# Attention over pooled keys and values, then four weighted experts: turning the probabilities on VectorE in 32x32 blocks, two heads as one element

## The chip, the cores and the metric

One core of a Trainium2 chip runs the whole program. The metric is device time in microseconds (us) from launch to end. The core has five engines that each work through a list of their own in order and wait for one another by semaphores: TensorE (PE; its weight loads are shown as PEld), VectorE (DVE), ScalarE (ACT), GpSimd (POOL) and SyncE (SP). POOL and SP issue the transfers between the memory of the chip (HBM) and the core. Matrix products are made in PSUM, all else lies in SBUF, which has 128 partitions.

## What is computed

```python
B, H, S, D = 8, 8, 576, 64                 # q, k, v; float32
k_p = k.reshape(B, H, 72, 8, D).mean(axis=3)
v_p = v.reshape(B, H, 72, 8, D).mean(axis=3)
scores = D ** -0.5 * (q @ k_p.transpose(0, 1, 3, 2))
attn = exp(scores - max(scores)); attn /= attn.sum() + 1e-9      # over the last axis
x = (attn @ v_p).transpose(0, 2, 1, 3).reshape(4608, 512)
p = domain_probs / (domain_probs.sum(-1) + 1e-9)                 # 4608 x 4
out = sum(p[:, e] * (relu(x @ w1[e]) @ w2[e]) for e in range(4)) # w1: 512 x 1024, w2: 1024 x 512
```

## The kernel before

The 4608 tokens are 36 tiles of 128; four tiles are a group of 512. An expert of a group is a *step*: 9 groups x 4 experts = 36 steps. A step has 12 *slots*, in threes: two slots with an `up` (L545, 4 products of 512 columns into `h_ps`, then a Relu on ScalarE, L549), always for the next step, and one slot with a `down` (L577, 8 products of 512 columns into `o_ps`) for one tile of this step, and its `collect` on VectorE (L592, or L588 for the first expert), which weighs `o_ps` and adds it to `acc`. `h_ps` and `o_ps` have two PSUM buffers each. The tiles of attention are done between these products: `plan` holds for each slot the functions to call after the slot's product, and `plan_tile` and `plan_batch` fill it. The order on every engine is the order in which the program calls things; no scheduler changes it.

For tile t, `due` is the first slot of its group and `base = due - 14` from tile 8 on. The functions and their slots after base are:

- `turn_q` (0): brings the queries to head dimension by token. From tile DT = 9 on this is VectorE's 32x32 transpose (L385) of `qblk`, which the load has already cut into blocks; earlier tiles do it on TensorE.
- `scores` (2): 4 products, one for each pair of heads, against `kT`, the turned sums of keys; head c and head c + 4 are a pair, on 64 partitions each. `less_max` (2) on VectorE: row maxima (L421) and their subtraction (L428).
- `expo` (4) on ScalarE (L446); it puts the heads back into order while it writes.
- `normalise` (5) on VectorE: row sums (L465), two short instructions (L454, L459), the product with the reciprocals into `ebuf` (L467), as bf16, 8 heads x 72 = 576 values a token.
- `turn_e` (8): TensorE turns `ebuf` in 5 blocks of 128 columns (the last one half empty) into `eT_ps` (L363), ScalarE copies them to `eT` (L364).
- `context_turned` (10): 8 products (L528) of `eT` with `vblk`, the sums of values spread with a mask so that each product gives the outputs of two neighbouring heads; then ScalarE's copy to `xT` (L533).

Tile 4 (`TPG`) to tile 7 are planned with other slots in steps 1 and 2, tiles 0 to 3 are written out by hand ahead of the steps. `gather_q` copies the queries of tiles 5 to 8 out of one wide load, in the slot ahead of their `turn_q`.

A batch has 576 tokens, 4.5 tiles. `plan_batch` spreads over slots, relative to the base of the first tile that needs the batch: `fold_k` twice and `end_k` (base - 6, - 5, - 4; sums of eight key rows on VectorE, L275 and L285, into `kpad`), `turn_k` (base - 2; TensorE, L304, then two copies, L312), `fold_v` twice, `end_v`, `spread_v` (base + 2 to + 5; L275, L325, L331). A load of the batch after next follows as soon as the buffer is free (`load_k`, `load_v`, L98; `load_qblk`, L149), all through POOL's queue. A tile that lies in two batches does its products in two segments.

Of the kernel before, what the change touches and what calls it, by code (L numbers as in the profile page):

```python
# [9 lines left out]
ACT = mybir.ActivationFunctionType  # L10
# [7 lines left out]
def kernel(  # L18
# [31 lines left out]
    NZ = 4  # L50
    BLK = 32
    PW = 2 * SP
    assert H * D == DM and D == 64 and SP == 72 and P == 128 and TAIL == 64

    const = ctx.enter_context(tc.tile_pool(name="const", bufs=1))
    wpool = ctx.enter_context(tc.tile_pool(name="wpool", bufs=1))
    raw = ctx.enter_context(tc.tile_pool(name="raw", bufs=1))
    prep = ctx.enter_context(tc.tile_pool(name="prep", bufs=2))
    qpool = ctx.enter_context(tc.tile_pool(name="qpool", bufs=8))
    qtpool = ctx.enter_context(tc.tile_pool(name="qtpool", bufs=TPG))  # L60
    qbpool = ctx.enter_context(tc.tile_pool(name="qbpool", bufs=2))
    soft = ctx.enter_context(tc.tile_pool(name="soft", bufs=2))
# [9 lines left out]
    ctx.enter_context(tc.manual_schedule())  # L72

    kraw = [raw.tile([P, NB, POOL * D], BF16, name=f"kraw{i}") for i in range(2)]
    vraw = [raw.tile([P, NB, POOL * D], BF16, name=f"vraw{i}") for i in range(2)]
    ebuf = [raw.tile([P, NB * P], BF16, name=f"ebuf{i}") for i in range(2)]
    w1_sb = [wpool.tile([P, KC, F], BF16, name=f"w1_{e}") for e in range(E)]
    w2_sb = [wpool.tile([P, FB, DM], BF16, name=f"w2_{e}") for e in range(E)]
# [22 lines left out]
        load_rows(nc.gpsimd, kraw[b % 2], rows_of(k[b]))  # L101

    def load_v(b):
        load_rows(nc.gpsimd, vraw[b % 2], rows_of(v[b]))

    def segments(t0, n):
        segs = []
        t = t0
        while t < t0 + n:
            b = t // S  # L110
            end = min(t0 + n, (b + 1) * S)
            segs.append((b, t - b * S, end - t, t - t0))
            t = end
        return segs


    qrow, qblk = {}, {}
# [26 lines left out]
    def load_qblk(b):  # L144

        qblk[b] = qbpool.tile([P, NPAIR * (S // BLK), BLK], BF16, name="qblk")
        for n32 in range(P // BLK):
            z, half = divmod(n32, 2)
            nc.gpsimd.dma_start(  # L149
                out=qblk[b][n32 * BLK:(n32 + 1) * BLK],  # L150
                in_=q[b][z * NPAIR:(z + 1) * NPAIR, :, half * BLK:(half + 1) * BLK]
                .rearrange("c (a i) j -> i (c a) j", i=BLK),
            )

    def load_w1(e, halves=(0, 1)):
        for half in halves:
# [11 lines left out]
            )  # L168

    qrun = raw.tile([P, 2, NPAIR, TPG, D], BF16, name="qrun")  # L170
    k0 = raw.tile([P, NB, POOL * D], F32, name="k0")
    load_rows(nc.sync, k0, rows_of(k[0]), ((NB - 1, NB), (0, 2), (2, NB - 1)))

    qg = raw.tile([P, H, TPG, D], F32, name="qg")
# [22 lines left out]
    for sign, base in ((1, PW), (-1, -SP - 1)):  # L197
        nc.gpsimd.affine_select(
            out=own[:], in_=own[:], compare_op=ALU.is_ge, fill=0.0,
            base=base, channel_multiplier=sign,  # L200
            pattern=[[sign * (P - PW), NB], [-sign * SP, NZ]],
        )
    gate = const.tile([1, 1], F32, name="gate")

# [36 lines left out]

    MZ = NZ - 1
    mask_v = const.tile([P, NB, MZ, D], BF16, name="mask_v")

    def spread_mask():
        nc.scalar.copy(
            out=mask_v[:], in_=own[:, :, 1:NZ].unsqueeze(3).to_broadcast([P, NB, MZ, D])
        )

    def domain_probs(probs, t0, t1):  # L250
        dsum = const.tile([P, t1 - t0], F32, name=f"dsum{t0}")
# [45 lines left out]
    def turn_k(b, odd=None, order=range(NB), between={}):  # L297

        flat = pads[b][:].rearrange("p i z d -> p (i z d)")
        ps = ps_t.tile([P, NB * P], BF16, tag="t", name="kT_ps")  # L300
        for i in order:

            n = P if i < NB - 1 or b > 0 else TAIL
            nc.tensor.transpose(  # L304
                ps[:, i * P:i * P + n], flat[0:n, i * P:(i + 1) * P], ident[0:n, 0:n]
            )
            if i in between:
                warm(between[i])
        kT[b] = kTs[b % 2]
        for z, copy in ((0, nc.scalar.copy), (1, odd or nc.scalar.copy)):  # L310
            half = slice(z * D, (z + 1) * D)
            copy(  # L312
                out=kT[b][half].rearrange("x (c z j) -> x z c j", z=2, j=SP)[:, z],
                in_=ps[half, 0:ROWS].rearrange("x (z c j) -> x z c j", z=2, j=SP)[:, z],
            )

    vsum = {}

    def fold_v(b, n):
        fold(vraw[b % 2], 0, NB, n)  # L320

    def end_v(b):
        rows = vraw[b % 2]
        vsum[b] = prep.tile([P, NB, D], BF16, name="v_sum")
        nc.vector.tensor_add(  # L325
            out=vsum[b][:], in0=rows[:, :, 0:D], in1=rows[:, :, D:2 * D]
        )

    def spread_v(b):
        vblk[b] = vblks[b % 2]  # L330
        nc.vector.tensor_tensor(  # L331
            out=vblk[b][:, :, 1:NZ],
            in0=vsum[b][:].unsqueeze(2).to_broadcast([P, NB, MZ, D]),
            in1=mask_v[:], op=ALU.mult,
        )
# [60 lines left out]
    def scores(t, halves=False):  # L396
        if halves:
            banks = [ps_h.tile([P, 512], F32, tag="h", name="sch")[:] for _ in range(2)]
            scs[t] = [(bank, slice(i, i + 1)) for i, bank in enumerate(banks)]
        else:  # L400
            sc = ps_s.tile([P, 2, 512], F32, name="sc")
            banks = [sc[:, 0, :], sc[:, 1, :]]
            scs[t] = [(sc[:].rearrange("p g x -> p (g x)"), slice(0, 2))]
        for b, _, n, at in segments(t * P, P):
            for pair in range(NPAIR):
                nc.tensor.matmul(  # L406
                    banks[pair // 2][at:at + n, (pair % 2) * PW:(pair % 2 + 1) * PW],
                    lhsT=qT[t][:, pair, at:at + n],
                    rhs=kT[b][:, pair * PW:(pair + 1) * PW],
                )  # L410

    maxima = {}
# [26 lines left out]
    def expo(t):  # L439

        if t < TPG:
            e = ebuf[t % 2][:, 0:ROWS]
        else:
            ef[t] = soft.tile([P, ROWS], F32, name="e_sb")
            e = ef[t][:]
        nc.scalar.activation(  # L446
            out=e.rearrange("p (z c j) -> p c z j", z=2, j=SP),
            in_=ds.pop(t)[:].rearrange("p g (c z) j -> p (g c) z j", z=2),
            func=ACT.Exp, scale=EXP_SCALE,
        )  # L450
# [11 lines left out]
    def normalise(t):  # L462
        e = ef.pop(t)[:].rearrange("p (h j) -> p h j", j=SP)
        total = soft.tile([P, H], F32, name="total")
        nc.vector.reduce_sum(out=total[:], in_=e, axis=AX.X)  # L465
        inverse(t, total[:])
        nc.vector.tensor_tensor(  # L467
            out=ebuf[t % 2][:, 0:ROWS].rearrange("p (h j) -> p h j", j=SP), in0=e,
            in1=es.pop(t)[:].unsqueeze(2).to_broadcast([P, H, SP]), op=ALU.mult,
        )  # L470

    def turn_e(t, copy=None):
        eT[t] = soft.tile([P, NB, P], BF16, name="eT")
        e = ebuf[t % 2]
        turned(eT[t][:], [e[:, i * P:(i + 1) * P] for i in range(NB)], "eT", copy)

# [44 lines left out]
    def context_turned(t):  # L523
        ps = ps_t.tile([P, KC, P], F32, tag="t", name="xT_ps")
        for b, _, n, at in segments(t * P, P):
            for pair in range(NPAIR):
                for i, z0 in ((pair, 2), (pair + 1, 0)):
                    nc.tensor.matmul(  # L528
                        ps[:, pair, at:at + n],
                        lhsT=vblk[b][:, i, z0:z0 + 2].rearrange("p z d -> p (z d)"),  # L530
                        rhs=eT[t][:, i, at:at + n], start=(z0 == 2), stop=(z0 == 0),
                    )
        nc.scalar.copy(out=x_columns(t), in_=ps[:])  # L533
# [95 lines left out]
    def plan_batch(b, slot, turn_slot, v_slot):  # L629
        at(slot, fold_k, b, 4)  # L630
        at(slot + 1, fold_k, b, 2)
        at(slot + 2, end_k, b)
        at(turn_slot, turn_k, b)
        at(v_slot, fold_v, b, 4)
        at(v_slot + 1, fold_v, b, 2)
        at(v_slot + 2, end_v, b)
        at(v_slot + 3, spread_v, b)
        if b + 2 < B:
            at(slot + 3, load_k, b + 2)
            at(v_slot + 3, load_v, b + 2)  # L640

    def plan_tile(t, base, steps):
        if TPG < t < DT:
            at(base - 1, gather_q, t)
        at(base, turn_q, t)
        at(base + steps[0], scores, t)
        at(base + steps[0], less_max, t)
        at(base + steps[1], expo, t)
        at(base + steps[2], normalise, t)
        at(base + steps[3], turn_e, t)  # L650
        at(base + steps[4], context_turned, t)
        return base + steps[4] + 1

# [3 lines left out]
    plan_batch(1, 3, 7, 18)  # L657
    for t in range(TPG, 2 * TPG):
        assert plan_tile(t, 12 + 3 * (t - TPG), (3, 5, 6, 9, 11)) <= 3 * SLOTS - 2
    last_b = 1  # L660
    for t in range(2 * TPG, NT):
        due = (t - TPG) * SLOTS
        base = due - 14
        b = ((t + 1) * P - 1) // S
        if b > last_b:
            plan_batch(b, base - 6, base - 2, base + 2)
            if 2 < b < B - 1:
                at(base + 1, load_qblk, b + 1)
            last_b = b
        assert plan_tile(t, base, (2, 4, 5, 8, 10)) <= due - 3  # L670

# [85 lines left out]
    down(0, 1)  # L759
    collect(0, 1)  # L760
    up_tile(0, 3, (0,))
    load_k(2)
    load_qblk(2)
    load_v(2)
# [46 lines left out]
```

## Time and profile before

| what | value |
|---|---|
| median of 3 runs | 560.41 us (560.26 to 561.49) |
| the profiled execution | 560.3 us |
| its span, first to last instruction | 558.6 us |
| mean granted TensorE clock | 0.999 |
| L545 `up` products | 270.4 us busy, 1084 recorded |
| L577 `down` products | 268.1 us busy, 1122 recorded |
| L363 transposes of probabilities, TensorE | 15.9 us busy, 180 |
| L528 products of the context | 19.6 us busy, 288 |
| L364 copy of turned probabilities, ScalarE | 24.1 us busy, 35 |
| period of an ordinary tile, collect to collect | 14.79 us (300.18 to 314.97) |

The span is what the profile sees; the time of a run has about 1.7 us around it. A matmul's recorded duration includes the way through the array and overlaps the next one, so counts times durations is more than the span; what a product costs TensorE is seen from the start of one to the start of the next. In a timeline each line has the start, the duration, the engine, the line of the program and, in square brackets, how long the engine sat idle before it and who released it.

### The profile page before, as it was taken

How to read it: one execution, taken by the hardware profiler on the slowest of the kernel's cores; microseconds unless marked ns; L12 is line 12 of the kernel's file. 1: busy time of each engine (PE TensorE's matmuls, PEld its weight loads, DVE VectorE, ACT ScalarE, POOL GpSimd, SP SyncE). 2: the span in 40 equal slices, each digit the busy share in tenths (PEclk: the TensorE clock that was granted, in tenths of full speed). 3: DMA queues.
4: the chain of work that ended last, by engine and by line, in shares of the span. 5: the costliest groups of instructions: out<-in, count | busy, mean ns of one | idle time of the engine just before them, and what ended most of it. 6: DMA issues, size and time to landing. Idle time of an engine off the chain costs nothing.

```text
span 558.6 us, 7696 instructions
## 1 busy us (share of the span) xinstructions
PE 547.1 (98%) x3187; PEld 277.6 (50%) x3245; DVE 275.7 (49%) x475; ACT 251.8 (45%) x435; POOL 62.5 (11%) x83
## 2 busy tenths in 40 slices
PE   7999999999999999999999999999999999999997
PEld 5854545444444445444444444544444444444444
DVE  5636846444654446544664444654456444422223
ACT  6744645444444444444444444544454444433330
POOL 6254331000400002200050003000000000000000
PEclk9999999999999999999999999999999999999999
DMA  9999996210690011901092019101000100001002
GB/s 221 207 200 206 182 158 138 43 5 0 105 100 0 2 56 40 108 0 39 38 97 33 19 58 38 6 1 62 14 2 0 47 31 0 1 38 39 0 1 76
DMA packets 87459, 33.67 MB, mean 60 GB/s; under 512 B 62080, under 2 KB 82368, under 8 KB 87424
## 3 DMA queue, kind: packets, MB, share of 16 engines
q0 software_dynamic: 75344, 21.43, 37.5%
q1 hardware_dynamic: 12080, 11.74, 6.2%
q8 instruction: 25, 0.41, 0.3%
q14 instruction: 10, 0.08, 0.1%
HBM read 45.16 MB, written 9.44 MB: 98 GB/s over the span
## 4 chain that ended last, share of the span: by engine, by line
PE 95%; DVE 3%; issue 1%; DMA 1%; SPq 0%; ACT 0%; ACTq 0%
PE o_ps L577 44%; PE h_ps L545 42%; PE xT_ps L528 3%; PE eT_ps L363 2%; PE sc L406 2%; PE h_ps L560 1%; DMA k<-in_k_dram 1%; DVE d_sb L428 1%; DVE mx L421 0%; PE kT_ps L304 0%; DVE k L275 0%; PE last_ps L610 0%; PE x_ps L497 0%; PE qT_ps L363 0%; DVE vraw L275 0%
## 5 line engine op out<-in xcount | busy, mean ns | idle before, releaser
L545 PE MATMUL h_ps<-xT,w 128*128 128x512 bf16 x1084 | 270.4, 379 | 1.6
L577 PE MATMUL o_ps<-w,h_sb 128*128 128x512 bf16 x1122 | 268.1, 379 | 1.2
L549 ACT ACTIVATE h_sb<-h_ps 128x512 bf16<-128x512 f32 x280 | 167.2, 597 | 224.0 <-PE h_ps L545 208.5
L577 PEld LDWEIGHTS <-h_sb 128*128 128x128 bf16 x1144 | 111.8, 98 | 134.2
L592 DVE SCALAR_TENSOR_TENSOR acc<-o_ps,p_sb,acc 128x512 f32<-128x512 f32 x107 | 80.3, 751 | 189.7 <-PE o_ps L577 186.7
L545 PEld LDWEIGHTS <-w 128*128 128x128 bf16 x1120 | 105.5, 98 | 109.5
L588 DVE TENSOR_SCALAR acc<-o_ps,p_sb 128x512 f32<-128x512 f32 x36 | 27.0, 750 | 68.9 <-PE o_ps L577 68.8
L533 ACT CAST xT<-xT_ps 128x512 bf16<-128x512 f32 x32 | 18.7, 585 | 50.3 <-PE xT_ps L528 50.3
L149 POOL DMA_DIRECT2D qblk<-in_q_dram x24 | 26.8, 1126 | 59.4 <-DVE qT L385 53.3
L421 DVE TENSOR_REDUCE mx<-sc 128x8 f32<-128x576 f32 x34 | 25.7, 756 | 8.3 <-PE sc L406 8.3
L98 POOL DMA_DIRECT2D kraw<-in_k_dram x14 | 9.2, 659 | 171.3 <-DVE kpad L285 165.4
L428 DVE TENSOR_TENSOR d_sb<-sc,mx 128x576 f32<-128x576 f32 x34 | 25.8, 757 | 1.2
L446 ACT ACTIVATE e_sb<-d_sb 128x576 f32<-128x576 f32 x32 | 21.8, 683 | 6.6 <-DVE d_sb L428 3.9
L467 DVE TENSOR_TENSOR ebuf<-e_sb,rs 128x576 bf16<-128x576 f32 x32 | 24.2, 758 | 1.1
L364 ACT COPY eT<-eT_ps 128x640 bf16<-128x640 bf16 x35 | 24.1, 687 | 1.2 <-PE eT_ps L363 1.2
L465 DVE TENSOR_REDUCE total<-e_sb 128x8 f32<-128x576 f32 x32 | 23.8, 744 | 0.4 <-ACT e_sb L446 0.4
L528 PEld LDWEIGHTS <-vblk 128*128 128x128 bf16 x288 | 17.3, 98 | 7.5
L528 PE MATMUL xT_ps<-eT,vblk 128*128 128x128 bf16 (+1 forms) x288 | 19.6, 213 | 0.0
L385 DVE STREAM_TRANSPOSE qT<-qblk 128x512 bf16<-128x512 bf16 (+1 forms) x30 | 19.1, 645 | 0.0
L363 PEld LDWEIGHTS <-ebuf 128*128 128x128 bf16 x180 | 12.9, 98 | 8.2 <-ACT ebuf L446 0.7
L363 PE MATMUL eT_ps<-ident,ebuf 128*128 128x128 bf16 x180 | 15.9, 219 | 0.2 <-ACT ebuf L446 0.2
L406 PEld LDWEIGHTS <-qT 128*128 128x128 bf16 (+1 forms) x160 | 11.1, 100 | 8.8 <-DVE acc L592 0.8
(77 smaller groups left out, 187.2 us busy)
## 6 DMA issues: line engine op xcount, KB each, us to landing
out_dram<-acc SPq DMA_DIRECT2D x35, 256.0 KB, 2.0
w<-in_moe_w_dram POOLq DMA_DIRECT2D x12, 512.0 KB, 14.0
vraw<-in_v_dram POOLq DMA_DIRECT2D x8, 512.0 KB, 6.6
kraw<-in_k_dram POOLq DMA_DIRECT2D x7, 512.0 KB, 6.8
qblk<-in_q_dram POOLq DMA_DIRECT2D x24, 144.0 KB, 7.1
w<-in_moe_w_dram POOLq DMA_DIRECT2D x2, 1024.0 KB, 17.7
k<-in_k_dram SPq DMA_DIRECT2D x2, 512.0 KB, 4.6
qg<-in_q_dram SPq DMA_DIRECT2D x2, 512.0 KB, 7.0
```

The source lines that it names most:

```text
L149: nc.gpsimd.dma_start(out=qblk[b][n32 * BLK:(n32 + 1) * BLK], in_=q[b][z * NPAIR:(z + 1) * NPAIR, :, half * BLK:(half + 1) * BLK] .rearran ...
L363: nc.tensor.transpose(ps[:, i, :], block, ident[:])
L364: (copy or nc.scalar.copy)(out=dst, in_=ps[:])
L421: nc.vector.reduce_max(out=mx[:], in_=view, axis=AX.X)
L428: nc.vector.tensor_tensor(out=ds[t][:, g], in0=view, in1=mx[:].unsqueeze(3).to_broadcast([P, n, 4, SP]), op=ALU.subtract,)
L467: nc.vector.tensor_tensor(out=ebuf[t % 2][:, 0:ROWS].rearrange("p (h j) -> p h j", j=SP), in0=e, in1=es.pop(t)[:].unsqueeze(2).to_broadcas ...
L528: nc.tensor.matmul(ps[:, pair, at:at + n], lhsT=vblk[b][:, i, z0:z0 + 2].rearrange("p z d -> p (z d)"), rhs=eT[t][:, i, at:at + n], start= ...
L545: nc.tensor.matmul(ps[:], lhsT=w1_sb[e][:, kc, fb * P:(fb + 1) * P], rhs=xT[g][:, kc, :], start=(kc == 0), stop=(kc == KC - 1),)
L549: nc.scalar.activation(out=hs[s][:, fb, :], in_=ps[:], func=ACT.Relu)
L577: nc.tensor.matmul(ps[:], lhsT=hs[s][:, fb, i * P:(i + 1) * P], rhs=w2_sb[e][:, fb, :], start=(fb == 0), stop=(fb == FB - 1),)
L588: nc.vector.tensor_scalar_mul(out=accs[t][:], in0=ps[:], scalar1=p_sb[:, e, t:t + 1])
L592: nc.vector.scalar_tensor_tensor(out=accs[t][:], in0=ps[:], scalar=p_sb[:, e, t:t + 1], in1=accs[t][:], op0=ALU.mult, op1=ALU.add,)
```

## The change

From tile 9 on, VectorE turns the probabilities, and TensorE and ScalarE no longer do.

- `normalise` writes `ehalf`: 288 rows of two values, the two being neighbouring heads (2s, 2s+1) at the same pooled key. Two bf16 values side by side are read as one 4-byte element. The row of 288 is made of 9 blocks of 32.
- `turn_e_part(t, a)` takes the 32 tokens 32a to 32a+31 and turns these blocks with four instructions. Instruction r takes the blocks r, r + 4, r + 8 and writes them to partitions 32r to 32r + 31: 3 blocks for r = 0, 2 for the others, 96 or 64 elements a partition. Four parts, 16 instructions a tile, in slots base + 6 to base + 9. `eT` is then 128 partitions x 3 chunks x 128 tokens x 2 heads.
- The order of the rows of values becomes that of the 288: `load_v` from batch 2 on brings them in four transfers (not two), two heads beside each other in the 6 (not 5) places of a partition; `fold_v` runs over 6 places, `end_v` sums to `v_half`, `spread_v` makes `vh` in four instructions (not one) with a new mask. The last place of a partition is cleared once by `clear_v`.
- `context_turned` still does 8 products for a segment: two for each pair of heads, with every second element of `eT` as the streamed operand.
- The pairs of heads change: in batches from 2 on, heads 4g + 2y and 4g + 2y + 1 share partitions of queries and keys. `load_qblk` takes 8 transfers (not 4), the copies in `turn_k` and the slices in `scores` follow, and `expo` writes its input in its order.
- From tile 9 on `base` is `due - 15` (before: 14), with steps (2, 4, 5, 6, 11), so that the context is at the same slot as before, and the batches' slots move with it. The gathers of tiles 5 to 8 move to slots 13 to 16 (before 14, 17, 20 and 33).
- Room: the buffer of the first keys, `k0`, is used again as `late`, which holds `ehalf`, `eTh` and `kTh`, two of each; six instructions of ScalarE clear parts of them and of `vh` in slots 2 to 7, four more spread the mask in slot 1, two clear the sixth place of `vraw`. `qpool` has 5 buffers, not 8.

```diff
@@ load_v @@
+        if b < WB:
+            load_rows(nc.gpsimd, vraw[b % 2], rows_of(v[b]))
+            return
+        rows = rows_of(v[b]).rearrange("(g y r) x -> r g y x", g=2, y=2)
+        to = vraw[b % 2][:].rearrange("p (c y) x -> p c y x", y=2)
+        n = HR // 2
+        for c, p0, g, r0, r1 in (
+            (0, 0, 0, 0, P), (1, 0, 0, P, n), (1, n - P, 1, 0, 2 * P - n),
+            (2, 0, 1, 2 * P - n, n),
+        ):
+            nc.gpsimd.dma_start(out=to[p0:p0 + r1 - r0, c], in_=rows[r0:r1, g])
@@ spread_v @@
+        if b >= WB:
+            vblk[b] = vh[b % 2]
+            for n, (c, g) in enumerate(SPAN):
+                z = n % 2
+                nc.vector.tensor_tensor(
+                    out=vblk[b][:, n, :, z:],
+                    in0=vsum[b][:, c].unsqueeze(2).to_broadcast([P, 2, 2 - z, D]),
+                    in1=mask_h[:, n, z:].unsqueeze(1).to_broadcast([P, 2, 2 - z, D]),
+                    op=ALU.mult,
+                )
+            return
@@ normalise @@
+        if t >= DT:
+            nc.vector.tensor_tensor(
+                out=ehalf[t % 2][:, 0:HR].rearrange("p (s j) y -> p s y j", j=SP),
+                in0=e.rearrange("p (s y) j -> p s y j", y=2),
+                in1=es.pop(t)[:].rearrange("p (s y) -> p s y", y=2).unsqueeze(3)
+                .to_broadcast([P, NPAIR, 2, SP]), op=ALU.mult,
+            )
+            return
@@ new @@
+    def turn_e_part(t, a):
+        eT[t] = eTh[t % 2]
+        toks = slice(a * BLK, (a + 1) * BLK)
+        src = ehalf[t % 2][toks].rearrange("p r y -> p (r y)").bitcast(F32)
+        for r in range(P // BLK):
+            rows = slice(r * BLK, (r + 1) * BLK)
+            dst = eT[t][rows].rearrange("p c k y -> p (c k y)").bitcast(F32)
+            n = -(-(NW - r) // 4)
+            nc.vector.transpose(
+                out=dst.rearrange("p (c k) -> p c k", k=P)[:, 0:n, toks],
+                in_=src.rearrange("p (c k) -> p c k", k=P)[:, 0:n, rows],
+            )
@@ context_turned @@
+            if t >= DT:
+                for pair in range(NPAIR):
+                    g, y = divmod(pair, 2)
+                    for m in (2 * g, 2 * g + 1):
+                        nc.tensor.matmul(
+                            ps[:, pair, at:at + n],
+                            lhsT=vblk[b][:, m, y].rearrange("p z d -> p (z d)"),
+                            rhs=eT[t][:, SPAN[m][0], at:at + n, y],
+                            start=(m == 2 * g), stop=(m == 2 * g + 1),
+                        )
+                continue
@@ plan_tile @@
-        if TPG < t < DT:
-            at(base - 1, gather_q, t)
...
-        at(base + steps[3], turn_e, t)
+        if t < DT:
+            at(base + steps[3], turn_e, t)
+        else:
+            for a in range(P // BLK):
+                at(base + steps[3] + a, turn_e_part, t, a)
@@ the plan @@
+    for t in range(TPG + 1, DT):
+        at(t + 8, gather_q, t)
...
-        base = due - 14
+        base = due - (15 if t >= DT else 14)
...
-        assert plan_tile(t, base, (2, 4, 5, 8, 10)) <= due - 3
+        steps = (2, 4, 5, 6, 11) if t >= DT else (2, 4, 5, 8, 10)
+        assert plan_tile(t, base, steps) <= due - 3
@@ ahead of the steps @@
+    late = early.tile([P, NB, POOL * D], F32, tag="k0", name="late")
...
+    zeros = [x for i in range(2) for x in (
+        kTh[i][:], eTh[i][:, 2], vh[i][:, 1::2, :, 0]
+    )]
+    for t in vraw:
+        nc.scalar.memzero(t[:, NB, :])
+    at(1, spread_mask_h)
+    for i, x in enumerate(zeros):
+        at(2 + i, nc.scalar.memzero, x)
```

More of the change, by code (lines that the diff above doesn't have):

```diff
@@ L52 @@
     PW = 2 * SP
+    WB = 2
+    HR = ROWS // 2
+    NW = HR // BLK
+    SPAN = ((0, 0), (1, 0), (1, 1), (2, 1))
     assert H * D == DM and D == 64 and SP == 72 and P == 128 and TAIL == 64
@@ L57 @@
     raw = ctx.enter_context(tc.tile_pool(name="raw", bufs=1))
+    early = ctx.enter_context(tc.tile_pool(name="early", bufs=1))
     prep = ctx.enter_context(tc.tile_pool(name="prep", bufs=2))
-    qpool = ctx.enter_context(tc.tile_pool(name="qpool", bufs=8))
+    qpool = ctx.enter_context(tc.tile_pool(name="qpool", bufs=5))
     qtpool = ctx.enter_context(tc.tile_pool(name="qtpool", bufs=TPG))
@@ L74 @@
     kraw = [raw.tile([P, NB, POOL * D], BF16, name=f"kraw{i}") for i in range(2)]
-    vraw = [raw.tile([P, NB, POOL * D], BF16, name=f"vraw{i}") for i in range(2)]
+    vraw = [raw.tile([P, NB + 1, POOL * D], BF16, name=f"vraw{i}") for i in range(2)]
+    ehalf, eTh, kTh = [], [], []
+    vh = [raw.tile([P, len(SPAN), 2, 2, D], BF16, name=f"vh{i}") for i in range(2)]
     ebuf = [raw.tile([P, NB * P], BF16, name=f"ebuf{i}") for i in range(2)]
@@ L103, in load_v @@
     def load_v(b):
-        load_rows(nc.gpsimd, vraw[b % 2], rows_of(v[b]))
+        if b < WB:
[9 more added lines that the diff above has]
+            nc.gpsimd.dma_start(out=to[p0:p0 + r1 - r0, c], in_=rows[r0:r1, g])
     def segments(t0, n):
@@ L147, in load_qblk @@
         for n32 in range(P // BLK):
[L148 to L153, printed above, removed]
+            y, half = divmod(n32, 2)
+            to = qblk[b][n32 * BLK:(n32 + 1) * BLK].rearrange("i (g c) d -> i g c d", g=2)
+            for g in range(2):
+                head = 4 * g + 2 * y
+                nc.gpsimd.dma_start(
+                    out=to[:, g],
+                    in_=q[b][head:head + 2, :, half * BLK:(half + 1) * BLK]
+                    .rearrange("z (a i) d -> i (z a) d", i=BLK),
+                )
     def load_w1(e, halves=(0, 1)):
@@ L170 @@
     qrun = raw.tile([P, 2, NPAIR, TPG, D], BF16, name="qrun")
-    k0 = raw.tile([P, NB, POOL * D], F32, name="k0")
+    k0 = early.tile([P, NB, POOL * D], F32, tag="k0", name="k0")
     load_rows(nc.sync, k0, rows_of(k[0]), ((NB - 1, NB), (0, 2), (2, NB - 1)))
@@ L201 @@
             pattern=[[sign * (P - PW), NB], [-sign * SP, NZ]],
+        )
+    ownh = const.tile([P, 3, 2, 2], BF16, name="ownh")
+    nc.gpsimd.memset(ownh[:], 1.0)
+    for sign, base in ((1, 0), (-1, SP - 1)):
+        nc.gpsimd.affine_select(
+            out=ownh[:], in_=ownh[:], compare_op=ALU.is_ge, fill=0.0,
+            base=base, channel_multiplier=sign,
+            pattern=[[sign * P, 3], [-sign * PW, 2], [-sign * SP, 2]],
         )
@@ L243 @@
     mask_v = const.tile([P, NB, MZ, D], BF16, name="mask_v")
+    mask_h = const.tile([P, len(SPAN), 2, D], BF16, name="mask_h")
     def spread_mask():
@@ L248, in spread_mask, with spread_mask_h @@
         )
+    def spread_mask_h():
+        for n, (c, g) in enumerate(SPAN):
+            nc.scalar.copy(
+                out=mask_h[:, n], in_=ownh[:, c, g].unsqueeze(2).to_broadcast([P, 2, D])
+            )
     def domain_probs(probs, t0, t1):
@@ L308, in turn_k @@
                 warm(between[i])
-        kT[b] = kTs[b % 2]
+        kT[b] = kTs[b % 2] if b < WB else kTh[b % 2]
         for z, copy in ((0, nc.scalar.copy), (1, odd or nc.scalar.copy)):
             half = slice(z * D, (z + 1) * D)
+            if b >= WB:
+                copy(
+                    out=kT[b][half, z].rearrange("x (g r) -> x g r", g=2),
+                    in_=ps[half, 0:ROWS].rearrange("x (g y r) -> x y g r", g=2, y=2)[:, z],
+                )
+                continue
             copy(
@@ L317, with clear_v @@
     vsum = {}
+    def clear_v(b):
+        nc.scalar.memzero(vraw[b % 2][BLK:TAIL, NB - 1, :])
     def fold_v(b, n):
-        fold(vraw[b % 2], 0, NB, n)
+        fold(vraw[b % 2], 0, NB if b < WB else NB + 1, n)
     def end_v(b):
         rows = vraw[b % 2]
+        if b >= WB:
+            vsum[b] = prep.tile([P, 3, 2, D], BF16, name="v_half")
+            nc.vector.tensor_add(
+                out=vsum[b][:].rearrange("p c y d -> p (c y) d"),
+                in0=rows[:, :, 0:D], in1=rows[:, :, D:2 * D],
+            )
+            return
         vsum[b] = prep.tile([P, NB, D], BF16, name="v_sum")
         nc.vector.tensor_add(
-            out=vsum[b][:], in0=rows[:, :, 0:D], in1=rows[:, :, D:2 * D]
+            out=vsum[b][:], in0=rows[:, 0:NB, 0:D], in1=rows[:, 0:NB, D:2 * D]
         )
     def spread_v(b):
+        if b >= WB:
+            vblk[b] = vh[b % 2]
+            for n, (c, g) in enumerate(SPAN):
+                z = n % 2
[4 more added lines that the diff above has]
+                    op=ALU.mult,
+                )
+            return
         vblk[b] = vblks[b % 2]
@@ L408, in scores @@
                     lhsT=qT[t][:, pair, at:at + n],
-                    rhs=kT[b][:, pair * PW:(pair + 1) * PW],
+                    rhs=kT[b][:, pair * PW:(pair + 1) * PW] if b < WB
+                    else kT[b][:, :, pair * SP:(pair + 1) * SP],
                 )
@@ L445, in expo @@
             e = ef[t][:]
+        if t >= DT:
+            nc.scalar.activation(
+                out=e, in_=ds.pop(t)[:].rearrange("p g h j -> p (g h j)"),
+                func=ACT.Exp, scale=EXP_SCALE,
+            )
+            return
         nc.scalar.activation(
@@ L466, in normalise @@
         inverse(t, total[:])
+        if t >= DT:
[4 more added lines that the diff above has]
+                .to_broadcast([P, NPAIR, 2, SP]), op=ALU.mult,
+            )
+            return
         nc.vector.tensor_tensor(
@@ L475, in turn_e @@
         turned(eT[t][:], [e[:, i * P:(i + 1) * P] for i in range(NB)], "eT", copy)
+    def turn_e_part(t, a):
[9 more added lines that the diff above has]
+                in_=src.rearrange("p (c k) -> p c k", k=P)[:, 0:n, rows],
+            )
     CHUNKS = ((0, 2, 4), (2, 0, 4), (4, 0, 2), (1, 1, 4), (3, 1, 4))
@@ L525, in context_turned @@
         for b, _, n, at in segments(t * P, P):
+            if t >= DT:
+                for pair in range(NPAIR):
[6 more added lines that the diff above has]
+                            start=(m == 2 * g), stop=(m == 2 * g + 1),
+                        )
+                continue
             for pair in range(NPAIR):
@@ L633, in plan_batch @@
         at(turn_slot, turn_k, b)
+        if WB <= b < WB + 2:
+            at(v_slot - 8, clear_v, b)
         at(v_slot, fold_v, b, 4)
@@ L761 @@
     up_tile(0, 3, (0,))
+    late = early.tile([P, NB, POOL * D], F32, tag="k0", name="late")
+    room = late[:].rearrange("p i x -> p (i x)").bitcast(BF16)
+    at0 = 0
+    for i in range(2):
+        for to, n, form in (
+            (ehalf, 6 * P, dict(pattern="p (r y) -> p r y", y=2)),
+            (kTh, 2 * HR, dict(pattern="p (y r) -> p y r", y=2)),
+            (eTh, 6 * P, dict(pattern="p (c k y) -> p c k y", c=3, y=2)),
+        ):
+            part = room[:, at0:at0 + n]
+            to.append(part.rearrange(form.pop("pattern"), **form))
+            at0 += n
+    zeros = [x for i in range(2) for x in (
[6 more added lines that the diff above has]
+        at(2 + i, nc.scalar.memzero, x)
     load_k(2)
```

## The prediction

> **What bounds the kernel now.** The first view is the page's table of engines, the second the busy time in a stretch in the middle of the run:
>
> ```profile
> span 558.6 us, 7696 instructions
> PE 547.1 (98%) x3187; PEld 277.6 (50%) x3245; DVE 275.7 (49%) x475; ACT 251.8 (45%) x435; POOL 62.5 (11%) x83
> 276.00:338.00 62.00, 61.63 (x350) 30.41 (x356) 32.45 (x54) 27.35 (x48) 7.10 (x8) 1.00 0.43 46
> ```
>
> TensorE is busy all the time at a granted clock of 1.00; VectorE and ScalarE work about half of it. So TensorE's list sets the end: work taken out of it counts fully, and so does any wait put into it. The third view is the timeline of one tile (start, duration, engine, line):
>
> ```profile
> 303.88 0.75 DVE L592 SCALAR_TENSOR_TENSOR acc<-o_ps,p_sb,acc 128x512 f32<-128x512 f32 x1 [1.04 <-PE o_ps L577]
> 304.55 0.74 DVE L465 TENSOR_REDUCE total<-e_sb 128x8 f32<-128x576 f32 x1
> 305.33 0.17 DVE L454 TENSOR_SCALAR s<-total 128x8 f32<-128x8 f32 x1
> 305.41 1.89 PE L577 MATMUL o_ps<-w,h_sb 128*128 128x512 bf16 x8
> 305.53 0.20 DVE L459 RECIPROCAL rs<-s 128x8 f32<-128x8 f32 x1
> 305.77 0.76 DVE L467 TENSOR_TENSOR ebuf<-e_sb,rs 128x576 bf16<-128x576 f32 x1
> 307.34 0.75 DVE L592 SCALAR_TENSOR_TENSOR acc<-o_ps,p_sb,acc 128x512 f32<-128x512 f32 x1 [0.81 <-PE o_ps L577]
> 308.00 0.44 PE L363 MATMUL eT_ps<-ident,ebuf 128*128 128x128 bf16 x5
> 308.28 1.03 PE L545 MATMUL h_ps<-xT,w 128*128 128x512 bf16 x4
> 308.69 0.69 ACT L364 COPY eT<-eT_ps 128x640 bf16<-128x640 bf16 x1
> ```
>
> Five transposes of probabilities hold TensorE from 308.00 to 308.28, where the next products start: 0.28 us. (A product of 512 columns takes 0.216 us from start to start: a `down` of 8 has 1.73, an `up` of 4 has 0.86.) A `collect` (L592) starts 0.20 after its `down` has issued its last product, 305.41 + 1.73 = 307.14.
>
> The fourth view is how close two VectorE instructions follow each other. First the rows by shape (count, busy us, mean ns), then lines of the timeline:
>
> ```profile
> L385 DVE STREAM_TRANSPOSE qT<-qblk 128x512 bf16<-128x512 bf16 x24 | 16.8, 701 | 0.0
> L385 DVE STREAM_TRANSPOSE qT<-qblk 128x256 bf16<-128x256 bf16 x6 | 2.3, 419 | 0.0
> 147.70 0.76 DVE L385 STREAM_TRANSPOSE qT<-qblk 128x256 bf16<-128x256 bf16 x2
> 9.57 0.71 ACT L376 CAST qrow<-qg 128x256 bf16<-128x256 f32 x2
> 9.70 0.31 DVE L312 COPY kT<-kT_ps 64x288 bf16<-64x288 bf16 x1 [0.86 <-ACT kT L312]
> 10.04 0.51 DVE L376 CAST qrow<-qg 128x256 bf16<-128x256 f32 x2
> ```
>
> Two transposes that need nothing of each other, 0.42 each, take 0.76 together: the second starts 0.08 before the first ends. The collect above (303.88 + 0.75) also overlaps `total` by 0.08. One that needs the other's result starts 0.03 after its end (304.55 + 0.74 to 305.33, roughly). The copy at 9.70 writes partitions 64 to 127, the cast behind it starts at partition 0 and needs nothing of it; its load had landed by 9.57, when ScalarE's cast of the same load began. Yet it starts 0.03 after the copy's end. It is the one pair here whose outputs start at different partitions, and it does not overlap.
>
> **The change, part by part.** All sums are made against the profiled execution, 560.3 us (span 558.6), which stands 0.1 below the median of 560.41.
>
> Removed: in tiles 9 to 35, 27 tiles, 5 transposes on TensorE, 27 x 0.28 = 7.5 us on the path, and ScalarE's copy of 0.69, which hid beside it and counts nothing. The products of the context stay 8 a tile.
>
> Added on VectorE: 16 transposes a tile, in four parts, one of 96 and three of 64 elements a partition in each. The two rows above give 137 ns + 1.10 ns an element: 243 and 207 ns. The price that matters is from start to start. Overlapped by 0.08 it is 163 and 127, a part of 0.54, a tile of 2.18. One after the other, with 0.03 between, it is 273 and 237, a part of 0.98, a tile of 3.94. Consecutive ones write partitions from 0, 32, 64 and 96 in turn, so the nearest row is the pair at 9.70, and I take 3.94. The ends for the range: with no operation under the 0.16 that those of 8 elements take, a serial one costs 0.19 (3.1 a tile); with a line through 0.163 at 8 elements and the slope of 1.10, 0.29 and 0.26 (4.3).
>
> The Trainium skill, "VectorE: DVE Perf Modes", section "Two Vector instructions with no wait between them", gives a model that says the same against this change: an instruction whose output starts in another group of 32 partitions than the last output is held until all earlier ones have finished. The pair at 9.70 agrees (+0.03 where others show -0.08); by that rule the sum is the serial one, without it the overlapped one of the rival below.
>
> An ordinary tile. In the new order TensorE has, from the end of the `down` at base+5 to the context at base+11, up, up, down twice: 2 x 3.45 = 6.90 us. In that time VectorE must start the collect (0.20 late), do it (0.67 to the next start), normalise (304.55 to 306.53, and 0.03: 2.01), do two parts, a collect (0.78), two parts, and hand over (0.04): 3.70 without the parts. Room for the 16: 3.20. Serial 3.94 misses it by 0.74; that is a wait of TensorE in each tile, larger than the 0.28 saved. Behind the context in TensorE's list stands everything, so nothing hides it.
>
> A tile in which the next batch's keys are folded (5 of them: batches 3 to 7; batch 2's fall into tile 8, which keeps the old way). The order of instructions is: part, fold of 1280 elements, part, fold of 640, collect, part, last sum, part; and `turn_k` stands in TensorE's list behind the second `up` after the second `down`, 5.18 us after the first one, so that 4.94 remain. The list up to the last sum (durations 0.82, 0.48, 0.49 from the rows of L275 and L285, 0.03 each): 0.67 + 2.01 + 3 x 0.98 + 0.85 + 0.51 + 0.78 + 0.52 = 8.28. TensorE waits 3.34 at the transposes of k. The fourth part then hides under the `down` that follows.
>
> A tile in which the values are folded (6). From 1280, 640 and 320 elements in 817, 483 and 315 ns I get 0.95, 0.55 and 0.35 for the 1536, 768 and 384 of the new layout. The first lies ahead of the row maxima and puts the second collect about 0.1 off; the four products with the mask (256, 128, 256, 128 elements; 0.28 and 0.21 by the rows of L331 and L325, overlapped) put 0.7 between collect and `total`: 0.8 more wait.
>
> Sum: -7.5 + 22 x 0.74 + 6 x 0.8 + 5 x 3.34 = -7.5 + 16.3 + 4.8 + 16.7 = +30.3: 590.6.
>
> Taken as nothing, with their bounds:
> - The early part. TensorE waited once for a gathered row, and the gathers move ahead of that: a gain of at most the 1.00 that this line shows. Against it stand ten more ScalarE instructions in slots 1 to 7 (zeros, the spread mask), where its Relus follow each other every 0.86 with 0.27 of rest: about 2.1 us in all by the rows of memzero and copy (0.29 to 0.43, overlapped by 0.1), if none of it hid.
>
> ```profile
> 56.75 0.40 PE L363 MATMUL qT_ps<-ident,qrow 128*128 128x128 bf16 x4 [1.00 <-DVE qrow L139]
> ```
>
> - The context's products read every second 2-byte element. No row shows it. Reads in runs of 64 (L342) take 219 ns at 128 columns as unbroken ones do (L528): nothing. The other end is half rate, 8 x 0.056 x 27 = 12. I see no way to a gain.
> - The exponentials and the product of `normalise` keep their 576 elements a partition; the latter writes every second 2-byte element, from float inputs that already come one at a time (758 ns).
> - POOL's queue: 8 transfers instead of 4 for a batch of queries, 4 instead of 2 for values, the same bytes. The waits of that queue are for buffers (165 us for `kpad`, 53 for `qT`), so loads start early. ScalarE's clearing of value rows ahead of a load moves it a slot at most.
>
> **The rivals.**
> - *The transposes overlap.* For it: every other independent pair; against it: the pair at 9.70. Then 2.18 fits into 3.20, the value tiles' 0.8 too, and only the k tiles wait: 0.67 + 2.01 + 3 x 0.54 + 0.74 + 0.40 + 0.67 + 0.49 = 6.60 against 4.94, 1.66 x 5 = 8.3. 560.3 - 7.5 + 8.3 = 561, from 558 to 563 with the early part.
> - *Faster.* The same, with shorter transposes: a quarter of the partitions and a stream of 64 to 96 elements could take less than the fixed 0.137. The k tiles decide: their wait is 5 x (1.66 - 12 x what a step is below 0.136), so under a mean step of 0.12 us the saving wins. At 0.09 it is 5 x 1.1 = 5.5, with most of the early gain: 557.5. Against it: no VectorE instruction here takes under 0.16.
> - *The stepped read costs half rate*: 12 more, 573 if the transposes overlap, 602 if not.
>
> **How the numbers follow.** Serial 0.58, overlapped 0.20, faster 0.15, stepped read 0.05, others (all slower) 0.02. Forecast: 590; the serial case alone runs from 570 (0.19 a step: no wait in ordinary tiles, 2.7 in the k tiles, 4 for values) to 601 (4.3 a tile). The range reaches down over the overlapped case: 557 to 600. Within 0.2% (1.1 us) is about what a measurement of this kernel can't tell from no change; the overlapped case is split 0.07 faster, 0.06 same, 0.07 slower. So faster 0.15 + 0.07 = 0.22, same 0.06, slower 0.58 + 0.07 + 0.05 + 0.02 = 0.72.
>
> **What would show it.** Right: starts of the transposes 0.24 to 0.27 apart with no overlap; the first product of the context idle about 0.7 in each tile with the transposes as releaser; the transposes of k idle about 3.3, five times, for `kpad`; periods of 15.2 us for an ordinary tile (14.79 now, 14.51 without any wait); PE's busy share near 93%. Wrong: starts 0.13 to 0.16 apart (overlapped; only k waits), or a context of more than 0.45 us from its first product to the next `up` (stepped read). If steps fall under 0.12, the forecast falls altogether.

## The result and the profile after

The change makes the kernel slower: 603.95 us (median of 4 runs, 603.14 to 606.2) against 560.53, a ratio of 1.078 with a 95% interval of 1.0756 to 1.0802. The profiled execution took 604.2, 43.9 more than the 560.3 of before; the spans differ by the same 43.9 (602.5 against 558.6). The mean granted clock is 0.986 (0.999 before).

The page's head and table of engines:

```profile
span 602.5 us, 7919 instructions
PE 552.8 (92%) x3055; PEld 272.8 (45%) x3110; DVE 383.7 (64%) x925; ACT 238.5 (40%) x422; POOL 81.7 (14%) x122
```

And rows by shape (count, busy us, mean ns):

```profile
L571 DVE STREAM_TRANSPOSE late<-late 32x64 f32<-32x64 f32 x324 | 76.8, 237 | 4.4
L571 DVE STREAM_TRANSPOSE late<-late 32x96 f32<-32x96 f32 x108 | 28.8, 267 | 2.3
L544 DVE TENSOR_TENSOR late<-e_sb,rs 128x576 bf16<-128x576 f32 x27 | 21.7, 805 | 1.0
```

TensorE has 132 recorded instructions less (5 x 27 = 135 were taken out), yet it rests 8% of the time. VectorE went from 276 to 384 us of work and is still free for a third of the span: it did not become the bound by its amount of work. The timeline of an ordinary tile shows where the rest comes from:

```profile
329.08 0.75 DVE L702 SCALAR_TENSOR_TENSOR acc<-o_ps,p_sb,acc 128x512 f32<-128x512 f32 x1 [1.50 <-PE o_ps L687]
329.75 0.74 DVE L541 TENSOR_REDUCE total<-e_sb 128x8 f32<-128x576 f32 x1
330.96 0.80 DVE L544 TENSOR_TENSOR late<-e_sb,rs 128x576 bf16<-128x576 f32 x1
331.80 2.04 DVE L571 STREAM_TRANSPOSE late<-late 32x96 f32<-32x96 f32 x8
333.86 0.75 DVE L702 SCALAR_TENSOR_TENSOR acc<-o_ps,p_sb,acc 128x512 f32<-128x512 f32 x1
334.06 1.89 PE L687 MATMUL o_ps<-w,h_sb 128*128 128x512 bf16 x7
334.63 2.06 DVE L571 STREAM_TRANSPOSE late<-late 32x96 f32<-32x96 f32 x8
336.74 0.62 PE L629 MATMUL xT_ps<-late,vh 128*128 128x128 bf16 x8 [0.79 <-DVE late L571]
337.20 1.89 PE L655 MATMUL h_ps<-xT,w 128*128 128x512 bf16 x8
```

VectorE's list has no gap from 329.08 to 336.69: collect, normalise, eight transposes in 2.04, collect, eight in 2.06. TensorE could have begun the context at 334.06 + 1.73 = 335.79 and began at 336.74: 0.95 of wait (the profile says 0.79 because a product's modelled end lies 0.16 behind the point at which the next could start). The eight products of the context then take 0.46 with their stepped reads, as they did before (8 x 0.056).

The timeline of a tile in which keys are folded:

```profile
296.24 1.89 PE L655 MATMUL h_ps<-xT,w 128*128 128x512 bf16 x8
300.86 0.49 DVE L325 TENSOR_TENSOR kpad<-kraw 128x640 bf16<-128x640 bf16 x1
301.40 0.45 PE L344 MATMUL kT_ps<-ident,kpad 128*128 128x128 bf16 x5 [3.27 <-DVE kpad L325]
301.69 3.15 PE L687 MATMUL o_ps<-w,h_sb 128*128 128x512 bf16 x8
304.64 1.06 PE L629 MATMUL xT_ps<-late,vh 128*128 128x128 bf16 x8
```

The busy time of each engine (PE first) in a stretch ahead of the wait, in the 3.4 us after it, and in the part of these in which the clock is down; the third column from the end, with 1.00, 0.61 and 0.50, is the granted clock:

```profile
294.50:298.00 3.50, 3.50 (x17) 1.47 (x15) 3.30 (x10) 1.20 (x2) 0.00 (x0) 1.00 0.00 0
301.40:304.80 3.40, 3.40 (x15) 1.51 (x16) 0.97 (x4) 0.79 (x2) 1.32 (x2) 0.61 0.38 46
302.16:305.57 3.41, 3.41 (x16) 1.76 (x15) 0.93 (x3) 0.52 (x2) 0.81 (x2) 0.50 0.66 92
```

TensorE waits from 297.97 to 301.40 for the last sum of keys, 3.43 us. And then the same `down` that has 1.73 everywhere else takes 2.95 from its start to the context's: from 302.16 on the granted clock is 0.50, for 3.41 us. So the wait costs more than its own length, 1.22 us more up to the context alone. The waits, summed (us in total, times, longest):

```profile
PE xT_ps L629 <- DVE late L571: 21.5, 22, 1.7
PE kT_ps L344 <- DVE kpad L325: 18.7, 7, 4.4
```

Of the 18.7, 17.5 belong to the five batches from 3 on (4.39, 3.30, 3.27, 3.28, 3.28). With 0.16 for each wait's modelled end, and a clock that took (1 - 0.986) x 602.5 = 8.4 us against 0.6 before (the trace has five stretches of 3.41 us at half clock, one behind each of these five waits), the difference is made of these terms:

| term | forecast | measured |
|---|---|---|
| TensorE's transposes gone | -7.5 | -7.5 |
| waits at the context, 22 tiles | 21.1 | 21.5 + 22 x 0.16 = 25.0 |
| waits at the transposes of k, 5 tiles | 16.7 | 17.5 + 5 x 0.16 = 18.3 |
| clock | 0 | 7.8 |
| sum | +30.3 | +43.6 (spans: +43.9) |

### The profile page after: what moved, and what is told of

Same layout as the page of the kernel before. It is cut to its first block, busy times and chain, and to the rows that moved or that the text cites. A ratio compares the mean times of both kernels' runs of the same rounds, so it can differ in the third digit from the quotient of the medians.

```text
span 602.5 us, 7919 instructions
## 1 busy us (share of the span) xinstructions
PE 552.8 (92%) x3055; PEld 272.8 (45%) x3110; DVE 383.7 (64%) x925; ACT 238.5 (40%) x422; POOL 81.7 (14%) x122
## 4 chain that ended last, share of the span: by engine, by line
PE 51%; DVE 39%; DMA 5%; issue 3%; POOL 1%; another core or an unknown queue 0%; SPq 0%; DVEq 0%
PE o_ps L687 24%; PE h_ps L655 21%; DVE late L571 16%; DVE acc L702 5%; DMA w<-in_moe_w_dram 4%; DVE late L544 4%; DVE total L541 3%; PE xT_ps L629 3%; DVE acc L698 2%; DVE vraw L315 1%; DVE d_sb L498 1%; DVE kraw L315 1%; DVE rs L535 1%; PE sc L475 1%; DVE mx L491 1%
## 5 line engine op out<-in xcount | busy, mean ns | idle before, releaser
L687 PE MATMUL o_ps<-w,h_sb 128*128 128x512 bf16 x1118 | 272.9, 386 | 0.9
L655 PE MATMUL h_ps<-xT,w 128*128 128x512 bf16 x1091 | 264.5, 379 | 2.5 <-DMA w<-in_moe_w_dram 0.3
L571 DVE STREAM_TRANSPOSE late<-late 32x64 f32<-32x64 f32 (+1 forms) x432 | 105.6, 244 | 6.7
L173 POOL DMA_DIRECT2D qblk<-in_q_dram x48 | 38.8, 819 | 75.6 <-DVE qT L454 60.6
L629 PE MATMUL xT_ps<-late,vh 128*128 128x128 bf16 (+1 forms) x240 | 18.2, 219 | 21.5 <-DVE late L571 21.5
L629 PEld LDWEIGHTS <-vh 128*128 128x128 bf16 x240 | 15.6, 100 | 32.4 <-issue 23.0
L544 DVE TENSOR_TENSOR late<-e_sb,rs 128x576 bf16<-128x576 f32 x27 | 21.7, 805 | 1.0
L344 PE MATMUL kT_ps<-ident,kpad 128*128 128x128 bf16 (+1 forms) x40 | 4.6, 250 | 18.7 <-DVE kpad L325 18.7
L517 ACT ACTIVATE e_sb<-d_sb 128x576 f32<-128x576 f32 x27 | 18.3, 677 | 2.5 <-DVE d_sb L498 2.5
L124 POOL DMA_DIRECT2D vraw<-in_v_dram x24 | 14.5, 613 | 12.7 <-DVE v_half L376 11.9
## 6 DMA issues: line engine op xcount, KB each, us to landing
w<-in_moe_w_dram POOLq DMA_DIRECT2D x2, 1024.0 KB, 18.3
```

The costliest lines, as they stand in the source:

```text
L173: nc.gpsimd.dma_start(out=to[:, g], in_=q[b][head:head + 2, :, half * BLK:(half + 1) * BLK] .rearrange("z (a i) d -> i (z a) d", i=BLK),)
L544: nc.vector.tensor_tensor(out=ehalf[t % 2][:, 0:HR].rearrange("p (s j) y -> p s y j", j=SP), in0=e.rearrange("p (s y) j -> p s y j", y=2), ...
L571: nc.vector.transpose(out=dst.rearrange("p (c k) -> p c k", k=P)[:, 0:n, toks], in_=src.rearrange("p (c k) -> p c k", k=P)[:, 0:n, rows],)
L629: nc.tensor.matmul(ps[:, pair, at:at + n], lhsT=vblk[b][:, m, y].rearrange("p z d -> p (z d)"), rhs=eT[t][:, SPAN[m][0], at:at + n, y], st ...
L655: nc.tensor.matmul(ps[:], lhsT=w1_sb[e][:, kc, fb * P:(fb + 1) * P], rhs=xT[g][:, kc, :], start=(kc == 0), stop=(kc == KC - 1),)
L687: nc.tensor.matmul(ps[:], lhsT=hs[s][:, fb, i * P:(i + 1) * P], rhs=w2_sb[e][:, fb, :], start=(fb == 0), stop=(fb == FB - 1),)
```

## The experiments

Three questions were open: whether the transposes really stand one after the other because of the partitions that they write; whether the clock falls because of the long waits at the transposes of k; and whether the saving of 7.5 us is there once the waits are gone. The first four kernels ran once each, with one run of before at 560.03 us beside them; the last two ran four times each, with runs of before of 560.17 us (median of 7). The first two leave the turned blocks in places in which the context does not want them, so they do not compute the attention and serve for times alone.

### Neighbours that keep their partitions

```diff
@@ turn_e_part: read and write one group, into columns of their own @@
-            dst = eT[t][rows].rearrange("p c k y -> p (c k y)").bitcast(F32)
+        dst = eT[t][toks].rearrange("p c k y -> p (c k y)").bitcast(F32)
...
-                out=dst.rearrange("p (c k) -> p c k", k=P)[:, 0:n, toks],
+                out=dst.rearrange("p (k j) -> p k j", j=BLK)[:, at0:at0 + n],
...
+            at0 += n
```

> Each part's four transposes write the group of 32 partitions that they read (part a: 32a to 32a+31), into columns of their own, so three of four neighbours keep both groups; the turned blocks lie in other places than the context wants them. Count, shapes and the waits of the list stay. Theory (an instruction whose output starts in another group of partitions than the last waits until that one is done): three of four steps overlap by 0.08 and fall from 0.24-0.30 to 0.16-0.19, a part from 1.02 to about 0.77, a tile from 4.10 to 3.1. The ordinary tiles' wait of 0.95 at the context goes, the value tiles' falls by 1.0, the k tiles' by 0.75: 604 - 25 = 579, and 570 if with that the five stretches at half clock go too. Rival (transposes of 32 partitions never overlap, whatever they write): steps stay 0.25, 604.

It took 567.0 us, less than either number of the theory. The rows of the transposes by shape:

```profile
L572 DVE STREAM_TRANSPOSE late<-late 32x64 f32<-32x64 f32 x324 | 48.4, 194 | 0.0
L572 DVE STREAM_TRANSPOSE late<-late 32x96 f32<-32x96 f32 x108 | 29.1, 270 | 2.3
```

And the four parts of an ordinary tile in its timeline:

```profile
312.08 1.31 DVE L572 STREAM_TRANSPOSE late<-late 32x96 f32<-32x96 f32 x8
313.40 0.75 DVE L704 SCALAR_TENSOR_TENSOR acc<-o_ps,p_sb,acc 128x512 f32<-128x512 f32 x1
314.16 1.32 DVE L572 STREAM_TRANSPOSE late<-late 32x96 f32<-32x96 f32 x8
```

Eight of the same instructions take 1.31 where they took 2.04: 0.16 a step, not 0.255, though the first of each part still changes its group. The trace's single starts show the same within this run: one that keeps its group starts 0.067 before the recorded end of the last one, one that changes it 0.013 after. A tile has 2.6 instead of 4.1, which fits into the room of 3.20, and no wait at a context is left; what remains above 560 is in the main the five waits at the transposes of k (2.04 four times, 3.14 once). So the spacing comes from the change of partitions, and the rival (such small transposes never overlap) falls.

### Reads that rotate, one group written

```diff
@@ as above, and the four instructions of a part read partitions from 0, 32, 64 and 96 @@
+            src = ehalf[t % 2][rows].rearrange("p r y -> p (r y)").bitcast(F32)
```

> As the run with one group, but within a part the four transposes read partitions from 0, 32, 64 and 96 in turn and write one group; the turned blocks lie in other places. If only the group written matters, as the one with one group: steps 0.16-0.19, 570 to 579. If the group read counts as well (the Trainium skill, VectorE: DVE Perf Modes, section 'Two Vector instructions with no wait between them', says that it does), steps stay 0.24 to 0.30 and the time 604.

The rows by shape:

```profile
L573 DVE STREAM_TRANSPOSE late<-late 32x64 f32<-32x64 f32 x324 | 76.6, 236 | 4.9
L573 DVE STREAM_TRANSPOSE late<-late 32x96 f32<-32x96 f32 x108 | 29.0, 269 | 2.3
```

603.7 us, and the rows are those of the change (76.6 and 29.0 us busy against 76.8 and 28.8). A change of the group that is read costs as much as one of the group that is written. It writes the same columns as the run before, so these are not what made the steps short there. That a change of the group read counts too is what the Trainium skill says ("VectorE: DVE Perf Modes", section "Two Vector instructions with no wait between them"). By these two runs no order of the 16 instructions of a tile would help: each has another pair of groups, so each step changes at least one.

### The sums of keys out of the way

```diff
-            plan_batch(b, base - 6, base - 2, base + 2)
+            plan_batch(b, base - 11, base - 2, base + 2)
```

> Only the three sums of keys of batches 2 to 7 move five slots earlier, out of the transposes' stretch into slots in which VectorE rests. Theory: the wait of 3.4 at the transposes of k goes (five tiles, which then wait 0.95 at the context as the others), and with it the five stretches of 3.4 at half clock, which it set off: 5 x 2.5 + 5 x 1.7 = 21 less, 583, clock 0.999. Rival for the clock (it falls because TensorE rests in many places, 0.95 in each tile): 12.4 less, 591.5, clock 0.986.

582.7 us, 21.3 less than the change, with a mean clock of 1.000. In the timeline, the transposes of k and the context of the same tile as above:

```profile
289.75 0.44 PE L344 MATMUL kT_ps<-ident,kpad 128*128 128x128 bf16 x5
...
292.44 0.63 PE L629 MATMUL xT_ps<-late,vh 128*128 128x128 bf16 x8 [0.51 <-DVE late L571]
```

The wait at the transposes of k is gone, one at the context (0.5 to 0.8 in these tiles, 1.65 in the first) has come in its place, and the 22 waits at the other contexts (0.8 to 1.7) are all still there. The clock is full all the same: the short waits do not lower it.

One slot earlier instead of five (`base - 7`):

> The three sums of keys move one slot earlier: the last sum then stands behind two parts and no collect. Theory: the wait at the transposes of k falls from 3.4 to 1.7 and the part that is left over falls on the context (two parts after the collect: about 1.9 less than the fold's time, near 0 to 1). No wait is long enough to halve the clock: 5 x 1.2 + 5 x 1.7 = 15 less, 589, clock 0.999. Rival (any wait of 1.5 or more halves it): 6 less, 598, clock 0.986.

One of its five such tiles in the timeline:

```profile
229.33 0.45 PE L344 MATMUL kT_ps<-ident,kpad 128*128 128x128 bf16 x5 [1.32 <-DVE kpad L325]
```

589.7 us, clock 1.000. Waits of 1.3 (1.5 with the modelled end) at the transposes of k leave the clock alone.

### Room for the transposes

```diff
-        base = due - (15 if t >= DT else 14)
+        base = due - (18 if t >= DT else 14)
...
-        steps = (2, 4, 5, 6, 11) if t >= DT else (2, 4, 5, 8, 10)
+        steps = (2, 4, 5, 6, 14) if t >= DT else (2, 4, 5, 8, 10)
```

> From tile 9 on each tile begins three slots earlier (base is due - 18) and its context stays where it was, so three slots later after base: the 16 transposes have 6.65 instead of 3.20 us of room. The keys are folded in the same place of the tile as in the change. Theory: the waits at the context go in all tiles (22 x 0.95 + 6 x 0.8 = 26), those at the transposes of k stay (four of 3.4, one of 4.5, and 1.7 each by the halved clock: 26.7): 560.3 - 7.5 + 26.7 = 579.5. Rival (VectorE has no time left and the waits move to the collects or the row maxima): 590 or more.

574.97 us, ratio to before 1.0252 (1.0230 to 1.0275). No wait at a context is left; five at the transposes of k are, of 3.3 each (batch 3's, too, which I had put at 4.5). The time is 4.5 below what was expected; 1.0 of it is that wait, and most of the rest the clock, whose mean is 0.991 in three of the four runs (0.009 x 573 = 5.2 us, not 8.5). Two of the five waits in the timeline:

```profile
222.87 0.45 PE L344 MATMUL kT_ps<-ident,kpad 128*128 128x128 bf16 x5 [3.30 <-DVE kpad L325]
284.68 0.45 PE L344 MATMUL kT_ps<-ident,kpad 128*128 128x128 bf16 x5 [3.27 <-DVE kpad L325]
```

And the busy times and the granted clock of the 3.4 us behind each (0.67 and 1.00), the later one first:

```profile
284.70:288.10 3.40, 3.40 (x15) 1.50 (x16) 1.30 (x5) 0.79 (x2) 1.32 (x2) 0.67 0.33 51
222.90:226.30 3.40, 3.40 (x20) 1.73 (x21) 2.14 (x6) 1.14 (x3) 3.19 (x5) 1.00 0.55 52
```

Two waits of the same length: behind the one the clock is 0.67, behind the other it stays at 1.00. The traces' records of the clock show what differs. In each of the eight traces the clock changes only at instants that lie whole multiples of 3.413 us apart, so the run can be cut into windows of that length. The two windows that the earlier wait lies in, then the one that holds most of the later wait, and the one behind it:

```profile
217.59:221.00 3.41, 1.98 (x10) 0.68 (x7) 3.25 (x10) 1.19 (x2) 0.00 (x0) 1.00 0.00 0
221.00:224.42 3.42, 1.55 (x11) 0.88 (x12) 2.71 (x10) 0.79 (x2) 1.31 (x3) 1.00 0.02 5
282.44:285.86 3.42, 1.19 (x10) 0.72 (x11) 3.08 (x10) 0.68 (x2) 0.95 (x2) 1.00 0.00 0
285.86:289.27 3.41, 3.41 (x10) 1.17 (x9) 1.43 (x3) 0.10 (x1) 0.51 (x2) 0.50 0.75 121
```

The earlier wait is split: TensorE rests 3.41 - 1.98 = 1.43 us of one window and 1.87 of the next, and the clock stays. The later one leaves it 3.42 - 1.19 = 2.23 us of rest in one window, and the next window runs at half clock. Over all eight traces this has no exception: behind each of the 13 windows at full clock with 2.15 us of rest or more the next is at half, and behind none with 2.00 or less. No run moved a wait against the windows on purpose.

### Both

The two edits together, nothing else:

> The context three slots later and the sums of keys five slots earlier, together. Theory: no wait is left and the 7.5 us of TensorE's transposes are won: 553, ratio 0.987, clock 0.999, ordinary period 14.51. Rival (VectorE, now some 12 of 14.5 us busy in a tile, holds up the subtraction of the maxima or a collect somewhere): 555 to 562.

The page's head and table of engines:

```profile
span 551.1 us, 7947 instructions
PE 541.0 (98%) x3056; PEld 270.4 (49%) x3110; DVE 384.2 (70%) x925; ACT 237.6 (43%) x422; POOL 81.7 (15%) x122
```

The parts of one tile in the timeline:

```profile
299.13 2.04 DVE L571 STREAM_TRANSPOSE late<-late 32x96 f32<-32x96 f32 x8
301.99 2.06 DVE L571 STREAM_TRANSPOSE late<-late 32x96 f32<-32x96 f32 x8
```

552.86 us (552.43 to 553.08), ratio to before 0.9859 (0.9841 to 0.9877): 1.4% less than before, a small gain that is clear of the noise. The transposes still take 2.04 and 2.06 for eight, and VectorE still does 384 us of work. What has changed is only when the results are wanted; TensorE is busy 98% of the time again, and the span is 7.5 below the 558.6 of before (7.3 by the medians beside it), about the price of the transposes that it no longer does.

## Why the prediction was wrong in size, and where it was right

- **The direction and the mechanism were right.** The forecast took the transposes as standing one after the other, by one pair of instructions in the trace of before (the copy at 9.70 and the cast at 10.04), against all the others that overlap. The run in which neighbours keep their partitions shows that this is the cause; where the transposes overlap there, the time drops to 567.
- **The step that failed** is the price of a wait at the transposes of k: "TensorE waits 3.34 at the transposes of k. The fourth part then hides under the `down` that follows." The wait has nearly that length (3.43 in four tiles), and the fourth part does hide. But the sum gives what follows the wait its price at full clock, and its list of what was taken as nothing does not name the clock at all: it took the 1.00 from a trace in which no wait of TensorE is longer than 1.7 us. Behind each of the five waits the clock was at half for 3.41 us. That missing term is 7.8 of the 13.3 us by which the sum of terms is short; without it the time would have been about 596, inside the range. The two runs that move the sums of keys show it: without those waits the mean clock is 1.000, though the 22 waits at the context are still there and five more have come.
- **Two terms were too small.** An ordinary tile waits 0.95 instead of 0.74: a transpose takes 237 and 267 ns where the line through two rows gave 207 and 243, so the 16 take 4.10 instead of 3.94, and the product of `normalise`, with its stepped writes, takes 805 ns, which I had taken as nothing above 758. Over 22 tiles, the value tiles among them, that is 3.9. The first k tile waits 4.55, because the domain probabilities of tiles 9 to 35 are worked out on VectorE in the same stretch (149.24 to 150.44), which I had not seen; it and the longer transposes make the 1.6 of the third term.
- **What else was taken as nothing** held where it can be read: the stepped reads cost nothing (0.46 for eight products); the early part neither gains nor loses, for the first 32x32 transpose of queries starts at 88.23 after and 88.27 before.
- **The range** of 557 to 600 missed the 604. Its upper end came from longer transposes alone (4.3 a tile gives 600 by the terms of the sum, not 601); the clock had no place in it. Of the rivals, the overlapped transposes (561) and the fast ones (557.5) both needed steps of at most 0.136, and the steps are 0.255; even where most transposes overlapped, in the run with one group, the mean step was 0.164 and the time 567.

## What to carry to other kernels

When work moves from the engine that sets the time to one that is half idle, do not ask whether the other engine has time, but when the bounding engine wants the result: sum the other engine's list, in order, from the point at which it can start to the point at which the result is wanted. Here 108 us of added work cost nothing once the same chain had 3.45 us more room and the sums of keys stood elsewhere, and the kernel 44 us while they had not. And a long wait of TensorE must be priced with the clock behind it: here the five waits of 3.3 to 4.4 us cost 7.8 us on top of their own length, while the waits of 2.04 us and less left the clock alone.

## What the runs showed of the hardware

- VectorE's transposes on 32 partitions stood 0.255 us apart where each changed the group of 32 that it read or wrote, and 0.16 where most kept both (eight in 2.04 and in 1.31 us).
- TensorE's clock changed, in all eight traces, only at instants whole multiples of 3.413 us apart. Behind each of the 13 windows of that length in which TensorE rested 2.15 us or more at full clock (five in the change, four with rotating reads, three with a later context, one with one group), the clock was at half for the next window, and behind no window with 2.00 or less. So 13 of 16 waits of 3.1 to 4.4 us were followed by half clock; the other three (3.30 and 3.28 with a later context, 3.28 with rotating reads) were split between two windows. Behind waits of 2.04 (four), 1.3 (five) and 0.8 it never fell. One stretch, with the later context, lasted two windows, with 0.83 us of rest in the first; why is open. The Trainium skill ("TensorE: Matmul & The Clock Gate", section "Part 1: The HAM clock gate (the "warmup" mystery)") gives a window of 3413 ns that runs on its own and does not start with the work; the spacing of the changes in these traces agrees with it.
- TensorE read every second 2-byte element of its streamed operand at full rate (eight products of 128 columns in 0.46 us; 8 x 0.056 = 0.45 before). VectorE's product took 805 ns where it wrote every second one, 758 before; no run changed that alone.
